# Two attention blocks on one core, planned by a list scheduler: a correction for every job, eviction and value round in the plan's ranking

## The chip, the cores and the metric

The kernel runs on one core of a Trainium2 chip. The metric is the device time in microseconds of one execution, the median of several runs. A profile of one execution stands beside it: its span is the time from the first to the last instruction of the program, and its own device time is a little longer.

## The reference

Two attention blocks of 2048 tokens, width 1024 and 32 heads of 32, in bf16, side by side in the output. The core of it, with the transposes left out:

```python
# A: plain attention over 2048 keys
qkv = x @ wqkv                                   # q, k, v: 32 heads x 2048 x 32
p = softmax(q @ k.T * Dh ** -0.5)
a = (p @ v) @ wo
# B: four segments of 512 with a memory carried along
for s in range(4):
    p = softmax(qs @ ks.T * scale + causal_mask)
    o = g * (phi(qs) @ M) / (phi(qs) @ z + 1e-6) + (1 - g) * (p @ vs)
    M = M + phi(ks).T @ vs;  z = z + phi(ks).sum()
b = concat(o) @ wo
out = concat(a, b)
```

## The kernel before

**Operations.** Attention A goes in 8 groups of 4 heads, each in 8 blocks of 256 queries; attention B in 4 segments, each in pairs of groups. The unit of work is a *set*: one tile of scores for each of 4 heads, 128 keys by 512 columns.

- A *row set* (L966) is the score matmuls of a set on TensorE (PE): four heads at a time in four row strips of the array. It is marked `urgent`.
- Two *exps* (L1042) on ScalarE (ACT) turn the set's scores into P, two tiles (1024 columns) at a time, from PSUM to a ring of 20 tiles in SBUF. `SLOT_BANKS` gives three slots of two PSUM banks; a set fills two slots, and each exp frees one.
- In about four of eight sets of a block (`SQUARES`) one of the four tiles takes another way: VectorE (DVE) writes Y (L1003), GpSimd (POOL) squares it into Pc (L1006), and the first exp has 512 columns only.
- A *value round* (`round`, L1133 and L1140) multiplies the tiles of a set by V and by ones, four heads at a time in four column strips: pairs of steps of 256 columns, which gather in one PSUM bank for a block. When an exp wants a tile of the ring, the last value step that reads the tile's old contents must have ended.
- A *norm* on DVE and POOL (L1191 to L1274) divides by the sums.
- *Jobs* are the projections: Q and K (`job_KA`, `job_KB`), V (`job_VA`, `job_VB`), outputs (`job_outA`, `job_outB`, and for the last rows `job_part`, `job_whole`, `job_last`), the memory of B (`job_phi`, `job_mem`, `job_M`) and some guards. A projection is eight steps of 512 columns (L599 is `mm4`, the helper that issues a step's four matmuls), each of which the plan may cut into two halves, and then an *eviction* by DVE (L1347). Jobs and value rounds share the PSUM banks 6 and 7 (`POOL_BANKS`).
- K and Q are squared on POOL (L1361) for a bound on the scores.

**Order.** Every operation is first recorded as an `Op` with its engine, a planned duration, a key (its wished place on a time axis in the plan), and its dependencies; `build` calls the recorded items in order of key. Then `Prog.schedule`, a list scheduler, plays all engines through and writes down one fixed order for each; `emit` sets the semaphores. Nothing is decided at run time but a guard against large scores. On each engine but PE, the ready operation with the smallest key comes first; what reads a group's PSUM bank has `XR` taken off its key, and an urgent operation that is ready soon enough (`SOON`) goes ahead. On PE, `pick` takes a row set when it is due (`ROW_LEAD`), and otherwise the operation with the smallest rank: for a value round its number `pvn` against the exps opened so far (`PV_ROOM`, `PV_T`, `PV_HOT`), for a job its key against the exps' progress (`JOB_AT`, `JOB_SLOPE`) or its due time (`DUE_AT`, `DUE_SLOPE`), with deductions for staying in one tiling mode (`STICK`) and for a group that is open (`XC`). A job is a candidate only up to `AHEAD` before its key. Weight loads go out from SyncE (SP), each gated by an exp.

```python
def rank(x):
    if x.pvn is not None:
        k = (x.pvn + PV_ROOM - st["opn"]) * PV_T if st["rows"] and x.need - st["opn"] > PV_HOT else -100.0
    else:
        k = JOB_AT + JOB_SLOPE * max(min(x.key - st["prog"], 20.0), -20.0)
        k = min(k, DUE_AT + DUE_SLOPE * (x.due - st["prog"]))
    if x.mode == mode:
        k -= STICK
    if x.grp is not None and x.pvn is None and not opens(x):
        k -= XC
    return k, x.key
```

Of the kernel before, what the change touches and what calls it, by code (L numbers as in the profile page):

```python
# [7 lines left out]
ACT = mybir.ActivationFunctionType  # L8
ALU = mybir.AluOpType
# [12 lines left out]
QC = 256  # L22
SLOT_BANKS = ((0, 1), (2, 3), (4, 5))
POOL_BANKS = (6, 7)
OL_LEAD, OL_MAX = 3.677, 7.166
P_RING = 20
Y_RING, C_RING = 3, 4
T_RING = 3
# [8 lines left out]
SQUARE_PV = 0.574  # L37
WHOLE = (("A", 7, 7), ("A", 7, 6))
BCK = 12.877
SOON = 0.596  # L40

PAIR = ((6, 0), (6, 1), (6, 2), (7, 0), (7, 1), (7, 2), (7, 3), (6, 3), (7, 4), (6, 4), (7, 5), (6, 5), (6, 6), (7, 6), (6, 7), (7, 7))
BIAS_PART = (17, 16, 18)
# [85 lines left out]
class Op:  # L129
    __slots__ = ("eng", "fn", "dur", "lat", "key", "mode", "svc", "deps", "order", "sem", "semval", "inc", "count",  # L130
                 "start", "end", "users", "ready", "urgent", "sched", "heat", "prog", "pvn", "margin", "pos", "due", "grp",
                 "gate", "alt", "flag", "redo", "need", "both")

    def __init__(self, eng, fn, dur, lat, key, mode=None, sem=None):
        self.eng, self.fn, self.dur, self.lat, self.key, self.mode, self.sem = eng, fn, dur, lat, key, mode, sem
# [9 lines left out]


LAT = {"PE": 0.22, "ACT": 0.29, "DVE": 0.10, "POOL": 0.15, "SP": 0.1}
SWITCH = 0.10
WIN = 3.413
ROW_LEAD = 2.689  # L150
AHEAD = 9.68
HEAT = 0.897
STICK = 0.28
OVER = 2.794
PV_ROOM = 6.219
PV_T = 1.014
PV_HOT = 1.215
NORM_K = 6.738
JOB_AT = 0.5
JOB_SLOPE = 0.572  # L160
MARGIN = 4.491
RXJ = 4
RX0 = 34.374
LEAD_A, LEAD_B, DUE_AT, DUE_SLOPE = 10.658, 3.249, 14.476, 0.203
HOLD = {}
BACKLOG = 3.378
XR = 9.514
XC = 2.115
STEP = 1.599
OUT3 = 90.167  # L170
OT_STEP = 3
NUDGE = {('KB', 3, 1): 15, ('VB', 1, 1): 4.2, ('OB', 0, 0): 5.05, ('OA', 1): 15, ('OB', 2, 0): 12, ('KB', 1, 0): 10.93, ('OA', 4): -21.65, ('KA', 5): -3.8, ('KB', 3, 2): 2.84, ('OA', 3): -6.14, ('OA', 5): 2.94, ('VB', 0, 0): -25, ('phi', 3, 1): 7.4, ('KB', 3, 3): 2.86, ('KB', 2, 2): -1.94, ('OA', 0): 4.63, ('VB', 2, 0): 8.32, ('phi', 0, 1): 2.89, ('KB', 1, 1): -15.35, ('phi', 1, 1): 2.05, ('phi', 3, 3): -0.06, ('VB', 1, 0): -1.48, ('OB', 0, 1): 8.97, ('VB', 2, 1): 3.43, ('OB', 3, 0): 6.01, ('VB', 3, 1): -7.84, ('OB', 1, 1): 2.06, ('OB', 1, 0): 6.22, ('KB', 1, 2): -2.71, ('phi', 0, 0): 4.5, ('VB', 0, 1): 10.96, ('OB', 3, 1): 7.23, ('phi', 2, 2): 5.96, ('KB', 2, 1): 13.45, ('VA', 1): -2.83, ('KA', 2): -0.38, ('KB', 2, 0): -4.38, ('phi', 2, 3): 0.21, ('phi', 3, 0): 0.15, ('phi', 0, 2): -2.66, ('phi', 1, 2): -2.16, ('phi', 2, 1): 5.51, ('OA', 2): 6.02, ('phi', 0, 3): -5.66, ('KB', 1, 3): -4.93, ('phi', 1, 0): 0.24, ('KB', 0, 1): 3.02, ('KB', 2, 3): -10.8, ('phi', 3, 2): 4.76, ('KA', 4): -4.63, ('phi', 1, 3): 15, ('KB', 0, 3): 10.75, ('KB', 0, 0): 3.13, ('VA', 3): -2.83, ('KB', 3, 0): -3.52, ('phi', 2, 0): -0.06, ('KA', 3): -0.02, ('OB', 2, 1): 6.93, ('VB', 3, 0): 0.3, ('KB', 0, 2): -0.5, ('KA', 6): -1.58}
SAFE = 0
WOA_STEP = 2
OUT_D = 66.251
M_AT = 1.576
# [6 lines left out]
class Prog:  # L183
    def __init__(self):
        self.ops = []
        self.due = 1e9
        self.before = {}

    def op(self, eng, fn, dur, key, reads=(), writes=(), mode=None, sem=None, lat=None, after=()):
        o = Op(eng, fn, dur, LAT[eng] if lat is None else lat, key, mode, sem)  # L190
        o.due = self.due
        for r in reads:
            for x in r.w:
                self._dep(o, x, True)
        for r in writes:
            for x in r.w:
                self._dep(o, x, False)
            for x in r.r:
                self._dep(o, x, False)
        for x in after:  # L200
            self._dep(o, x, True)
        for r in reads:
            r.r.append(o)
        for r in writes:
            r.w, r.r = [o], []
        for g in {r.grp for r in (*reads, *writes) if r.grp is not None}:
            o.grp = g
            if eng == "PE" and g.pe:
                o.order.add(g.pe[0])
            (g.pe if eng == "PE" else g.rd).append(o)  # L210
        self.ops.append(o)
        return o
# [13 lines left out]
    def schedule(self):  # L226
# [11 lines left out]
        for o in self.ops:  # L238
            al = o.deps | o.order | {x for x, _ in o.gate}
            pend[o] = len(al)  # L240
            for x in al:
                x.users.append(o)
        exps = {o: n for n, o in enumerate(o for o in self.ops if o.prog)}
        for o in self.ops:
            if o.pvn is not None:
# [14 lines left out]
        last = {b: list(r.w) + list(r.r) for b, r in self.before.items()}  # L260
# [45 lines left out]
        def pick(t, av, c):  # L306
            mode = st["mode"]
            row = [x for x in av if x.urgent]
            nxt = [x for x in c if x.urgent]
            due = max(min((x.ready for x in nxt), default=1e9), st["act_end"] - ROW_LEAD) if nxt else 1e9  # L310
            if row and t >= due - 0.02:
                return min(row, key=lambda x: x.key)
            slack = due - t
            cold = heat(t, 2.6) < HEAT * 2.6
            def rank(x):
# [9 lines left out]
                return k, x.key  # L325
            av = [x for x in av if not x.urgent and (x.pvn is not None or x.key <= st["prog"] + AHEAD or cold)]
            first = [min((x for x in av if opens(x) and x.grp.sums is v), key=rank, default=None) for v in (False, True)]
            best = None
            for x in av:
                if opens(x) and x not in first:  # L330
                    continue
                d = x.dur + (SWITCH if x.mode != mode else 0.0)
                v = (d > slack + OVER, *rank(x))
                if best is None or v < best[0]:
# [9 lines left out]
        while left:  # L344
            best = None
            for e, c in cand.items():
                if c:
                    t = max(free[e], min(x.ready for x in c))
                    if best is None or t < best[0]:
                        best = (t, e)  # L350
            t, e = best
            c = cand[e]
            av = [x for x in c if x.ready <= t + 1e-9]
            if e == "PE":
                av = [x for x in av if not opens(x) or opening(x)[0] <= t + 1e-9]
                o = pick(t, av, c)
                if o is None:
# [6 lines left out]
                    o = min((x for x in c if x.ready <= t + 1e-9 and (not opens(x) or opening(x, True)[0] <= t + 1e-9)), key=lambda x: x.key)  # L364
            else:
                if e == "SP" and st["dma"] - t > BACKLOG:
# [5 lines left out]
                    c = av  # L372
                o = min((x for x in c if x.ready <= t + HOLD.get(e, 0.0)), key=lambda x: x.key - (XR if x.grp is not None else 0.0))
                soon = min((x for x in c if x.urgent), key=lambda x: x.ready, default=None)
                if soon is not None and soon.ready < max(t, o.ready) + o.dur - SOON:
                    o = soon
                t = max(t, o.ready)
            d = o.dur
            if e == "PE":
                ck = clock(t)  # L380
                d /= ck
                if o.mode != st["mode"]:
                    t += SWITCH
                st["mode"] = o.mode
# [182 lines left out]
class _Kernel:  # L567
# [63 lines left out]
    def build(self):  # L631
        nc = self.nc
        with ExitStack() as es:
            self.es = es
            self.alloc()
            self.items = []
            self.exps, self.exp_keys = [], []
            self.plan()
            self.items.sort(key=lambda x: (x[0], x[1]))
            for key, _, f in self.items:  # L640
                f(key)
            self.pg.before = {b: self.bank[b] for b in POOL_BANKS}
            self.pg.schedule()
            run = self.pg.emit(nc, es, None, self.out_sems + self.sm_last)
            block = es.enter_context(nc.Block())

            @block.gpsimd
            def _(eng):
                run("POOL", eng)

            @block.sync
            def _(eng):
                run("SP", eng)

            @block.tensor
            def _(eng):
                run("PE", eng)

            @block.scalar
            def _(eng):  # L660
                run("ACT", eng)

            @block.vector
            def _(eng):
                run("DVE", eng)
# [325 lines left out]
    def plan_square(self, t, bank, T):  # L991

        i, k = self.nsquare % Y_RING, self.nsquare % C_RING
        self.nsquare += 1
        Y, rY = self.Y[i], self.r_Y[i]
        dst, rP = self.Pc[:, k, :], self.r_Pc[k]
        t["P"] = (self.Pc, k, rP)
        bc = t["bias"]
        last = []

        def f(key):
            src = self.ps[:, 512 * bank:512 * bank + 512]
            o = self.dve(lambda e: e.tensor_scalar(Y[:, :], src, KAPPA * SCALE, BETA, ALU.mult, ALU.add), 512, key - 9.0,  # L1003
                         [self.bank[bank]], [rY], fixed=0.15)
            o.urgent = True
            last.append(self.pool(lambda e: e.tensor_tensor(dst, Y[:, :], Y[:, :], ALU.mult), 512, key - BCK, [rY], [rP], rate=0.435))  # L1006
        self.item(T + 0.001, f)
        return (lambda e: e.activation(dst, Y[:, :], ACT.Exp, bias=self.bias[:, 60 + bc:61 + bc], scale=1.0 / KAPPA),
                bc, rY, rP, last, t)
# [347 lines left out]
    def square(self, kind, src, rsrc, key):  # L1357
        i = self.nsq[kind] % 4
        self.nsq[kind] += 1
        sq, rs = self.sq[kind][i], self.r_sq[kind][i]  # L1360
        self.pool(lambda e: e.tensor_tensor(sq[:, :], src, src, ALU.mult), 512, key, [rsrc], [rs], rate=0.5)  # L1361
        return sq, rs

    def guard_cols(self, key, sqs, bank=None, urgent=None, wide=512):
# [648 lines left out]
```

## Time and profile before

| | |
|---|---|
| time, median of 3 runs | 1090.2 us (1090.05 to 1095.13) |
| profiled execution | 1089.23 us, its span 1087.5 us |
| granted TensorE clock | 0.999 |
| PE busy (matmuls) | 1027.5 us, 25410 instructions |
| ACT busy | 1030.8 us, 1224 instructions |
| DVE busy | 734.4 us, 1648 instructions |
| POOL busy | 575.3 us, 653 instructions |
| exps (L1042) | 1176, 1001.5 us |

Busy times are the union of an engine's instructions in the profiled execution; matmuls are pipelined, so PE's share is not a share of its peak. In rows of a timeline the columns are start and duration in us, engine, line, operation, out<-in, shapes and count, with the idle time before and what ended it in brackets. In rows of groups they are busy us and mean ns of one, then the idle time before and its releasers. In rows of waits they are the total in us, how often, and the longest.

### The profile page before, as it was taken

How to read it: one execution, taken by the hardware profiler on the slowest of the kernel's cores; microseconds unless marked ns; L12 is line 12 of the kernel's file. 1: busy time of each engine (PE TensorE's matmuls, PEld its weight loads, DVE VectorE, ACT ScalarE, POOL GpSimd, SP SyncE). 2: the span in 40 equal slices, each digit the busy share in tenths (PEclk: the TensorE clock that was granted, in tenths of full speed). 3: DMA queues.
4: the chain of work that ended last, by engine and by line, in shares of the span. 5: the costliest groups of instructions: out<-in, count | busy, mean ns of one | idle time of the engine just before them, and what ended most of it. 6: DMA issues, size and time to landing. Idle time of an engine off the chain costs nothing.

```text
span 1087.5 us, 56100 instructions
## 1 busy us (share of the span) xinstructions
PE 1027.5 (94%) x25410; PEld 560.7 (52%) x25410; DVE 734.4 (68%) x1648; ACT 1030.8 (95%) x1224; POOL 575.3 (53%) x653
## 2 busy tenths in 40 slices
PE   8999999999999999998989999999999999999998
PEld 4555555655545544465445544466555545445554
DVE  2346587578585587887685598786865697774444
ACT  4999999999999999998999999999999999999997
POOL 2213575457564475756456476665646567554311
PEclk9999999999999999999999999999999999999999
DMA  9032251016223240033212241042112551021201
GB/s 196 22 88 56 65 139 31 9 16 121 52 63 100 69 97 20 13 59 85 56 50 80 66 107 23 15 95 55 47 34 71 134 191 42 31 68 45 67 27 51
DMA packets 171391, 72.18 MB, mean 66 GB/s; under 512 B 134800, under 2 KB 169360, under 8 KB 171152
## 3 DMA queue, kind: packets, MB, share of 16 engines
q1 hardware_dynamic: 168784, 67.79, 25.4%
q8 instruction: 200, 3.28, 1.3%
q10 hardware_dynamic: 2368, 0.79, 0.3%
q14 instruction: 39, 0.32, 0.1%
HBM read 45.29 MB, written 11.73 MB: 52 GB/s over the span
## 4 chain that ended last, share of the span: by engine, by line
PE 62%; ACT 21%; DVE 11%; issue 2%; SPq 2%; DMA 1%; POOL 0%; ACTq 0%; DVEq 0%
PE ps L599 31%; ACT P L1042 20%; PE ps L966 12%; PE ps L1133 9%; PE ps L1140 8%; DVE Y L1003 2%; SPq L1312 2%; DVE T L1191 1%; PE ps L1602 1%; DVE PKQ_B L1651 1%; ACT PKQ_B L1646 1%; DVE KQ_B L1347 1%; DMA xT_A<-in_A_x_dram 1%; DVE rc L1202 1%; DVE T L1197 1%
## 5 line engine op out<-in xcount | busy, mean ns | idle before, releaser
L1042 ACT ACTIVATE P<-ps 128x1024 bf16<-128x1024 f32 (+1 forms) x1176 | 1001.5, 996 | 36.8 <-PE ps L1140 16.1
L1006 POOL TENSOR_TENSOR Pc<-Y 128x512 bf16<-128x512 f32 x226 | 238.5, 1055 | 255.1 <-DVE Y L1003 102.3
L1140 PE MATMUL ps<-P,onesb 128*32 128x256 bf16 (+1 forms) x4412 | 295.0, 270 | 0.3 <-issue 0.3
L1133 PE MATMUL ps<-P,V_A 128*32 128x256 bf16 x3644 | 252.4, 274 | 4.6 <-DVE T L1197 1.3
L966 PE MATMUL ps<-KQ_A 32*128 32x256 bf16 x4096 | 204.0, 273 | 18.5 <-ACT P L1042 10.3
L1003 DVE TENSOR_SCALAR Y<-ps 128x512 f32<-128x512 f32 x226 | 154.4, 683 | 79.8 <-PE ps L966 73.1
L966 PEld LDWEIGHTS ps<-KQ_A 32*128 32x128 bf16 x4096 | 61.9, 92 | 161.3 <-ACT P L1042 99.6
L599 PE MATMUL ps<-xT_B,W_B 128*32 128x512 bf16 (+1 forms) x2244 | 138.6, 362 | 4.6 <-DVE OT_B L1672 1.6
L1140 PEld LDWEIGHTS ps<-P,onesb 128*32 128x32 bf16 x4412 | 129.2, 97 | 24.5 <-issue 9.5
L599 PE MATMUL ps<-xT_A,W_A 128*32 128x512 bf16 (+1 forms) x2224 | 138.1, 364 | 3.7 <-DMA xT_A<-in_A_x_dram 1.1
L1133 PEld LDWEIGHTS ps<-P,V_A 128*32 128x32 bf16 x3644 | 107.7, 96 | 36.4 <-issue 11.9
L1133 PE MATMUL ps<-Pc,V_A 128*32 128x256 bf16 x452 | 112.9, 273 | 0.4 <-ACT P L1042 0.2
L1140 PE MATMUL ps<-Pc,onesb 128*32 128x256 bf16 x452 | 113.2, 273 | 0.0
L1361 POOL TENSOR_TENSOR sqA<-KQ_A 128x512 bf16<-128x512 bf16 x61 | 64.7, 1063 | 85.8 <-DVE KQ_A L1347 44.2
L1065 POOL TENSOR_SCALAR_AFFINE_SELECT P<-P 128x768 bf16<-128x768 bf16 (+1 forms) x96 | 77.7, 814 | 48.0 <-ACT P L1042 47.0
L1361 POOL TENSOR_TENSOR sqB<-KQ_B 128x512 bf16<-128x512 bf16 x64 | 68.1, 1063 | 38.6 <-DVE KQ_B L1347 27.7
L1191 DVE STREAM_TRANSPOSE T<-ps 128x256 f32<-128x256 f32 (+1 forms) x148 | 71.8, 486 | 23.6 <-PE ps L1140 19.5
L599 PEld LDWEIGHTS ps<-xT_B,W_B 128*32 128x32 bf16 x2244 | 51.5, 96 | 55.8 <-issue 23.3
L599 PEld LDWEIGHTS ps<-xT_A,W_A 128*32 128x32 bf16 x2224 | 51.7, 96 | 50.2 <-issue 15.3
L1347 DVE CAST KQ_A<-ps 128x512 bf16<-128x512 f32 x60 | 41.1, 686 | 48.6 <-PE ps L599 48.6
L1213 DVE STREAM_TRANSPOSE T<-rc 128x256 f32<-128x256 f32 (+1 forms) x152 | 71.6, 477 | 1.8
L1347 DVE CAST outsb<-ps 128x512 bf16<-128x512 f32 x56 | 38.4, 686 | 50.2 <-PE ps L599 40.7
(113 smaller groups left out, 1305.8 us busy)
## 6 DMA issues: line engine op xcount, KB each, us to landing
Wv_B<-in_B_wv_dram SPq DMA_DIRECT2D x32, 256.0 KB, 3.2
W_B<-in_B_wk_dram SPq DMA_DIRECT2D x32, 256.0 KB, 3.2
W_B<-in_B_wq_dram SPq DMA_DIRECT2D x32, 256.0 KB, 3.8
Wo_B<-in_B_wo_dram SPq DMA_DIRECT2D x32, 256.0 KB, 3.0
out_dram<-outsb SPq DMA_DIRECT2D x56, 128.0 KB, 1.8
W_A<-in_A_wqkv_dram SPq DMA_DIRECT2D x14, 256.0 KB, 3.2
ot_a_scratch<-OTst SPq DMA_DIRECT2D x51, 64.0 KB, 1.9
xT_A<-ot_a_scratch SPq DMA_DIRECT2D x6, 512.0 KB, 4.7
```

The lines of the kernel that those rows point to most:

```text
L599: ins = e.matmul(out[r], w[:, r], x, start=start, stop=stop, tile_position=(0, 32 * t), skip_group_check=True)
L966: ins = e.matmul(out, kap, qap, start=st, stop=True, tile_position=(32 * h, 0), skip_group_check=True)
L1003: o = self.dve(lambda e: e.tensor_scalar(Y[:, :], src, KAPPA * SCALE, BETA, ALU.mult, ALU.add), 512, key - 9.0, [self.bank[bank]], [rY], f ...
L1006: last.append(self.pool(lambda e: e.tensor_tensor(dst, Y[:, :], Y[:, :], ALU.mult), 512, key - BCK, [rY], [rP], rate=0.435))
L1042: a = self.act(guarded if early else lambda e: e.activation(dst, src, ACT.Exp, scale=SCALE), cols, key, rd, wr, fixed=EXP_FIXED)
L1065: self.pool(lambda e: e.affine_select(v, v, pattern=pat, compare_op=ALU.is_ge, fill=0.0, base=0, channel_multiplier=-1), 2 * nd * P, key + ...
L1133: ins = e.matmul(self.pb(obk, q0, q0 + nq, slice(32 * h, 32 * h + 32)), v, p, start=first, stop=last, tile_position=(0, 32 * h), skip_grou ...
L1140: ins = e.matmul(self.pb(obk, QC + q0, QC + q0 + nq, slice(32 * h, 32 * h + 32)), self.onesb[:, 0:32], p, start=False, stop=last, tile_pos ...
L1191: self.dve(lambda e: e.transpose(T2[:, 0:n], src()), n, nk, rsrc, [r2], fixed=0.17)
L1213: self.dve(lambda e: e.transpose(T2[:, 0:n].rearrange("p (b r) -> p b r", r=32), bc), n, key, [rr], [r2], fixed=0.17)
L1347: self.dve(lambda e: e.tensor_copy(dst, src()), 512, key, [self.at(b)], rdst, fixed=0.155)
L1361: self.pool(lambda e: e.tensor_tensor(sq[:, :], src, src, ALU.mult), 512, key, [rsrc], [rs], rate=0.5)
```

## The change

Two things change in what the planner is given, and nothing in what is computed. Every recorded `Op` gets the number of the item that made it, and before the scheduling starts a table `SHIFT`, with 1638 entries by item and engine, is added to its key, or for a value round to its number `pvn`; row sets and exps have none. Seventeen of the planner's constants get other values, and two planned rates of POOL's squares go from 0.435 and 0.5 to 0.56 elements per ns. The counts of operations on every engine stay the same; twelve projection steps more than before are issued as two halves.

```diff
-OL_LEAD, OL_MAX = 3.677, 7.166
+OL_LEAD, OL_MAX = 4.319064149904418, 41.00003697785312
-SOON = 0.596
+SOON = 0.5905590911714352
-ROW_LEAD = 2.689
-AHEAD = 9.68
-HEAT = 0.897
-STICK = 0.28
-OVER = 2.794
-PV_ROOM = 6.219
-PV_T = 1.014
-PV_HOT = 1.215
+ROW_LEAD = 10.450797042452189
+AHEAD = 122.90457192896793
+HEAT = 2.917270822004343
+STICK = -2.216533454202848
+OVER = 9.83100976449197
+PV_ROOM = 6.511791041192874
+PV_T = 1.226406207969171
+PV_HOT = 1.9091538080027601
-JOB_AT = 0.5
-JOB_SLOPE = 0.572
+JOB_AT = 1.1168622049752417
+JOB_SLOPE = 1.811535016666137
-LEAD_A, LEAD_B, DUE_AT, DUE_SLOPE = 10.658, 3.249, 14.476, 0.203
+LEAD_A, LEAD_B, DUE_AT, DUE_SLOPE = 10.658, 3.249, 49.75785267190463, 1.9998068229774686
-XR = 9.514
-XC = 2.115
+XR = 67.02011029255661
+XC = 2.943398126899734
+SHIFT = {(n, e): v for e, t in (
+    ("POOL", {
+        3: -0.5, 4: 1.5, 5: 0.25, 6: 3, 8: 1.75, 10: -4.5, 11: -0.5, 12: 2.75, 13: 3.25, 15: 0.5, 16: 1.25, 17: 5.5,
...
+) for n, v in t.items()}
@@ Prog.op
         o.due = self.due
+        o.item = self.item
@@ Prog.schedule, ahead of everything that uses a key
+        for o in self.ops:
+            if o.pvn is not None:
+                o.pvn += SHIFT.get((o.item, o.eng), 0.0)
+            elif not o.prog and (o.urgent is None or o.eng != "PE"):
+                o.key += SHIFT.get((o.item, o.eng), 0.0)
@@ _Kernel.build
-            for key, _, f in self.items:
+            for key, n, f in self.items:
+                self.pg.item = n
                 f(key)
@@ plan_square
-            last.append(self.pool(lambda e: e.tensor_tensor(dst, Y[:, :], Y[:, :], ALU.mult), 512, key - BCK, [rY], [rP], rate=0.435))
+            last.append(self.pool(lambda e: e.tensor_tensor(dst, Y[:, :], Y[:, :], ALU.mult), 512, key - BCK, [rY], [rP], rate=0.56))
@@ square
-        self.pool(lambda e: e.tensor_tensor(sq[:, :], src, src, ALU.mult), 512, key, [rsrc], [rs], rate=0.5)
+        self.pool(lambda e: e.tensor_tensor(sq[:, :], src, src, ALU.mult), 512, key, [rsrc], [rs], rate=0.56)
```

More of the change, by code (lines that the diff above doesn't have):

```diff
@@ L131 @@
                  "start", "end", "users", "ready", "urgent", "sched", "heat", "prog", "pvn", "margin", "pos", "due", "grp",
-                 "gate", "alt", "flag", "redo", "need", "both")
+                 "gate", "alt", "flag", "redo", "need", "both", "item")
     def __init__(self, eng, fn, dur, lat, key, mode=None, sem=None):
@@ L147 @@
 LAT = {"PE": 0.22, "ACT": 0.29, "DVE": 0.10, "POOL": 0.15, "SP": 0.1}
-SWITCH = 0.10
+SWITCH = 0.1
 WIN = 3.413
-ROW_LEAD = 2.689
-AHEAD = 9.68
-HEAT = 0.897
-STICK = 0.28
-OVER = 2.794
-PV_ROOM = 6.219
-PV_T = 1.014
-PV_HOT = 1.215
+ROW_LEAD = 10.450797042452189
[6 more added lines that the diff above has]
+PV_HOT = 1.9091538080027601
 NORM_K = 6.738
-JOB_AT = 0.5
-JOB_SLOPE = 0.572
+JOB_AT = 1.1168622049752417
+JOB_SLOPE = 1.811535016666137
 MARGIN = 4.491
@@ L172 @@
 NUDGE = {('KB', 3, 1): 15, ('VB', 1, 1): 4.2, ('OB', 0, 0): 5.05, ('OA', 1): 15, ('OB', 2, 0): 12, ('KB', 1, 0): 10.93, ('OA', 4): -21.65, ('KA', 5): -3.8, ('KB', 3, 2): 2.84, ('OA', 3): -6.14, ('OA', 5): 2.94, ('VB', 0, 0): -25, ('phi', 3, 1): 7.4, ('KB', 3, 3): 2.86, ('KB', 2, 2): -1.94, ('OA', 0): 4.63, ('VB', 2, 0): 8.32, ('phi', 0, 1): 2.89, ('KB', 1, 1): -15.35, ('phi', 1, 1): 2.05, ('phi', 3, 3): -0.06, ('VB', 1, 0): -1.48, ('OB', 0, 1): 8.97, ('VB', 2, 1): 3.43, ('OB', 3, 0): 6.01, ('VB', 3, 1): -7.84, ('OB', 1, 1): 2.06, ('OB', 1, 0): 6.22, ('KB', 1, 2): -2.71, ('phi', 0, 0): 4.5, ('VB', 0, 1): 10.96, ('OB', 3, 1): 7.23, ('phi', 2, 2): 5.96, ('KB', 2, 1): 13.45, ('VA', 1): -2.83, ('KA', 2): -0.38, ('KB', 2, 0): -4.38, ('phi', 2, 3): 0.21, ('phi', 3, 0): 0.15, ('phi', 0, 2): -2.66, ('phi', 1, 2): -2.16, ('phi', 2, 1): 5.51, ('OA', 2): 6.02, ('phi', 0, 3): -5.66, ('KB', 1, 3): -4.93, ('phi', 1, 0): 0.24, ('KB', 0, 1): 3.02, ('KB', 2, 3): -10.8, ('phi', 3, 2): 4.76, ('KA', 4): -4.63, ('phi', 1, 3): 15, ('KB', 0, 3): 10.75, ('KB', 0, 0): 3.13, ('VA', 3): -2.83, ('KB', 3, 0): -3.52, ('phi', 2, 0): -0.06, ('KA', 3): -0.02, ('OB', 2, 1): 6.93, ('VB', 3, 0): 0.3, ('KB', 0, 2): -0.5, ('KA', 6): -1.58}
-SAFE = 0
+SAFE = 0.0
+SHIFT = {(n, e): v for e, t in (
+    ("POOL", {
[42 rows of a table added]
+    ("DVE", {
[132 rows of a table added]
+    ("ACT", {
[3 rows of a table added]
+) for n, v in t.items()}
 WOA_STEP = 2
@@ L186, in __init__ @@
         self.due = 1e9
+        self.item = 0
         self.before = {}
```

176 rows, old and new, of the table SHIFT are left out of this document.

## The prediction

> **What bounds the kernel now.** I read the page first: its busy shares, slices, chain and costliest group.
>
> ```profile
> span 1087.5 us, 56100 instructions
> ...
> PE 1027.5 (94%) x25410; PEld 560.7 (52%) x25410; DVE 734.4 (68%) x1648; ACT 1030.8 (95%) x1224; POOL 575.3 (53%) x653
> ...
> PE   8999999999999999998989999999999999999998
> ACT  4999999999999999998999999999999999999997
> PEclk9999999999999999999999999999999999999999
> ...
> PE 62%; ACT 21%; DVE 11%; issue 2%; SPq 2%; DMA 1%; POOL 0%; ACTq 0%; DVEq 0%
> ...
> L1042 ACT ACTIVATE P<-ps 128x1024 bf16<-128x1024 f32 (+1 forms) x1176 | 1001.5, 996 | 36.8 <-PE ps L1140 16.1 <-PE ps L966 14.1 <-PE ps L1602 1.4
> ```
>
> ACT and PE are both nearly full all the time, at an undisturbed clock, and the chain changes between them: they run in lockstep. PSUM has three slots of two banks; a row set (L966) fills two of them and two exps (L1042) empty them, so PE can be ahead of ACT by a fraction of one exp only. No instruction is added or taken away by the change, so ACT's 1030.8 us of work stay. What can go are ACT's waits. The sums by stretch say how many there are away from both ends:
>
> ```profile
> 50.00:1075.00 1025.00, 975.07 (x24356) 533.89 (x24344) 713.46 (x1599) 991.27 (x1181) 562.44 (x611) 1.00 0.25 64
> ```
>
> 1025.00 - 991.27 = 33.7 us. The waits of ACT say on what (total, times, longest):
>
> ```profile
> ACT P L1042 <- PE ps L1140: 16.1, 28, 1.3
> ACT P L1042 <- PE ps L966: 14.1, 36, 2.5
> ACT KQ_A L1517 <- PE ps L599: 8.1, 1, 8.1
> ACT P L1029 <- DVE flags L1450: 3.5, 1, 3.5
> ACT P L1042 <- PE ps L1133: 1.1, 1, 1.1
> ```
>
> Two kinds count. An exp waits for its **row set** (L966, 14.1 us): PE came to it too late. Or it waits for a **value round** (L1140 and L1133, 17.2 us): the exp writes a tile of the ring P, and the round that still reads this tile stands further back in PE's order. The 8.1 and 3.5 us belong to the start; both programs are alike there (PE's first 171 steps, to the ninth row set). The timeline around 460 us shows the second kind.
>
> ```profile
> 459.86 2.18 ACT L1042 ACTIVATE P<-ps 128x1024 bf16<-128x1024 f32 x2
> ...
> 460.57 0.40 PE L966 MATMUL ps<-KQ_A 32*128 32x256 bf16 x8
> 460.90 1.26 PE L599 MATMUL ps<-xT_A,W_A 128*32 128x512 bf16 x20
> 461.99 0.28 PE L1133 MATMUL ps<-P,V_A 128*32 128x256 bf16 x4
> 462.10 0.28 PE L1140 MATMUL ps<-P,onesb 128*32 128x256 bf16 x4
> ...
> 462.31 0.40 PE L966 MATMUL ps<-KQ_A 32*128 32x256 bf16 x8
> 462.64 0.29 PE L1133 MATMUL ps<-P,V_A 128*32 128x256 bf16 x3
> ...
> 462.98 0.28 PE L1140 MATMUL ps<-P,onesb 128*32 128x256 bf16 x3
> ...
> 463.31 1.02 ACT L1042 ACTIVATE P<-ps 128x1024 bf16<-128x1024 f32 x1 [1.27 <-PE ps L1140]
> ```
>
> After the row set at 460.57 PE does five projection steps, a pair of value steps, the next row set, and only then the value steps that free the tile. The second exp of the set of 460.57 stands still for 1.27 us, though its scores were ready long before.
>
> The same rows give prices. Five projection steps (20 matmuls of 512 columns) take from 460.90 to 461.99, 0.218 each; a value step (four matmuls of 256 columns) takes 461.99 to 462.10, 0.11; a row set 462.31 to 462.64, 0.33, and about 0.11 between the last value step's share and its start, so 0.44. The exps:
>
> ```profile
> 29.05 1.02 ACT L1042 ACTIVATE P<-ps 128x1024 bf16<-128x1024 f32 x1
> 40.10 4.69 ACT L1042 ACTIVATE P<-ps 128x1024 bf16<-128x1024 f32 x5 [0.16 <-PE ps L1140]
> L1042 ACT ACTIVATE P<-ps 128x1024 bf16<-128x1024 f32 x950 | 924.6, 1078 | 30.4 <-PE ps L1140 14.3 <-PE ps L966 9.9 <-PE ps L1602 1.4
> L1042 ACT ACTIVATE P<-ps 128x512 bf16<-128x512 f32 x226 | 146.4, 648 | 6.4 <-PE ps L966 4.2 <-PE ps L1140 1.8
> ```
>
> One alone shows 1.02, five in a row 4.69: (4.69 - 1.02) / 4 = 0.917 from start to start. The 512-column one is shorter by 1078 - 648 ns, so 0.487.
>
> **The change part by part.** I laid the two programs' orders side by side and counted in both with these prices; no clock of the plan enters.
>
> *Value rounds.* For each exp I took the value step that frees its tile and summed PE's steps between the exp's own row set and that step; it is late where the sum is over 0.2 us (a first exp; from the row set's end at 460.90 to its exp at about 461 lies a little less) or 0.2 plus the first exp's length (a second exp). Before: 48 exps late, 19.8 us together, 1.5 of it in one set of the start. The trace has 17.2 us, and the late places are those of its long waits (the one above is counted at 1.05). After: 20 late, 6.7 us, the same 1.5 included. At the places that hold six of the long waits of before, the freeing step now stands ahead of the next row set. Scaled, 17.2 x 6.7 / 19.8 = 5.8 stay: **-11.4 us**. The best case is that only the start's 1.5 stay, -15.7; the worst is rival 2.
>
> *Jobs and row sets.* Between two row sets PE has what ACT takes from the end of one set's first exp to the end of the next set's: 0.917 + 0.917, or 0.917 + 0.487 where the next set has a square, and a phi exp if one lies there. I summed PE's steps in each of 582 gaps (those of the start left out) with 0.44 for the row set. The mean gap is 0.06 us under ACT's time in both orders, but the spread is smaller after (standard deviation 0.34 before, 0.26 after). What exceeds ACT's time by over 0.3 us, counted beyond the 0.3: before 65 gaps with 14.9 us, after 36 with 5.2. All excess: before 46.1, after 25.9. The first count is near the measured 14.1, the second far above, so I take the first: 14.1 x 5.2 / 14.9 = 4.9 stay, **-9.2 us**. By the second 7.9 would stay, -6.2; none can give more than -14.1.
>
> *The end.* It grows.
>
> ```profile
> 1078.38 1.47 PE L599 MATMUL ps<-V_A,xT_A 128*32 128x512 bf16 x24
> 1080.21 0.61 PE L599 MATMUL ps<-V_A,xT_A 128*32 128x512 bf16 x8
> 1080.64 2.52 PE L599 MATMUL ps<-W_A,xT_A 128*32 128x512 bf16 x40
> 1081.64 0.42 DVE L1252 TENSOR_TENSOR xT_A<-ps,T 128x256 bf16<-128x256 f32 x1
> ```
>
> The last output sums have fourteen steps; six (the row at 1078.38) stand ahead of the last value steps and eight behind them, from 1080.21. Then come four that need what DVE delivers at 1082.06 (1081.64 + 0.42). Eight at 0.218 end at 1081.95: just hidden. In the new order an output job stands behind the last row set and pushes these steps back: two are ahead of the last value steps, twelve behind, and one of job_last among them. Thirteen end at 1080.21 + 2.83 = 1083.04. An eviction now stands in the last normalisation on DVE too; it moves DVE's end by less than that. **+1.0 us**; from 0 to +1.7.
>
> *The rest.* The two planning rates of POOL (0.435 and 0.5, now 0.56 elements per ns) alter no instruction. They tell the plan 512 / 0.56 + 150 = 1064 ns for a square, where the row has 1055; the old 0.435 gave 1327.
>
> ```profile
> L1006 POOL TENSOR_TENSOR Pc<-Y 128x512 bf16<-128x512 f32 x226 | 238.5, 1055 | 255.1 <-DVE Y L1003 102.3 <-PE ps L599 60.0 <-ACT P L1042 24.6
> ...
> PE ps L599 <- issue: 2.7, 2, 2.4
> ...
> PE ps L1372 <- POOL P L1065: 0.4, 1, 0.4
> ...
> W_B<-in_B_wq_dram SPq DMA_DIRECT2D x32, 256.0 KB, 3.8
> ```
>
> Twelve more projection steps are cut into halves of 256 columns; the halves cost what the whole does. Openings of the two shared banks (6 and 7) that come before the eviction is over are 42 instead of 50 by the same count. The weight loads of B take 3.8 us to land (the row above) and by the order still have at least a set's time, some 1.7 us, to spare. One stall of 2.4 us within a job waits for nothing in the order; I leave it in and give it to the range.
>
> Sum: -11.4 - 9.2 + 1.0 = -19.6. The profiled execution took 1089.2 (1.7 outside its span), 1.0 under the median of 1090.2; the sum is relative, so 1090.2 - 19.6 = 1070.6.
>
> **The rivals.**
>
> *1. PE becomes the bound.* 0.06 us x 592 sets is 36 us of room on PE, hardly more than ACT's 33.7 us of waits. If drains that my prices miss eat it, the row sets stay as late as they are, and -11.4 + 1.0 gives 1079.8. For it: PE's 94%. Against it: ACT's row waits came from single long gaps, not from all. The Trainium skill (Perfetto Trace Analysis, Identifying the Most-Contended Engine) judges PE's room by its weight-load share and not by matmul busy time; by the 52% here this rival would give nothing back. The trace bears out that busy time misleads, but not a room of half: the gaps have 0.06 us.
>
> *2. The ring is too small, not badly ordered.* Twenty tiles of P stay twenty. If PE frees tiles later than its order says, the waits for value rounds only move, and -9.2 + 1.0 gives 1082.0. Against it: the count by order hits the waits of before one by one. The Trainium skill (Perfetto Trace Analysis, Optimization Strategy) has this rule: the same gap again and again on the engine that should be full can mean that SBUF has too few buffers. By it the 17.2 us stay. The trace shows 29 waits on nearly 1200 exps, not a steady gap.
>
> *3. Slower: squares come late to PE.* The value steps of a squared tile wait for POOL. Those within three sets of their row set are 70 instead of 58, which is 35 squares at two pieces each. PE takes its steps in order, so each late square stops the row sets behind it. Late by one POOL instruction each, 35 x 1.055 = 37 us are added: 1107.5. It outweighs the gain from 19 such squares on. Against it: PE's waits in the trace have no row for Pc, only 0.4 us for POOL, at a similar spacing, and POOL is 53% busy.
>
> *4. Nothing changes.* The plan's order is right for the plan's clock only, and waits appear elsewhere (banks, loads) as fast as they go: about 1090. Against it: I counted with measured prices.
>
> **How the numbers follow.** Forecast 0.62, rival 1 0.12, rival 2 0.13, rival 3 0.06, rival 4 0.07. Low end: the ring's best case, -15.7 - 9.2 + 1.0, and the 2.4 us stall gone: 1063.9. High end: rival 2 with one more such stall, 1084.4. So 1064 to 1084 leaves out rivals 3 and 4 and a little of the others. What a measurement of this kernel can tell is about 0.5%, 5.5 us: the forecast and rivals 1 and 2 are faster by more (0.87), rival 4 is the same (0.07), rival 3 slower (0.06).
>
> **What would show it.** In ACT's waits after: L1140 and L1133 together near 6 us (rival 2: near 17), L966 near 5 (rival 1: near 14), ACT's busy time unchanged near 1031. In the timeline of the end: the last four projection steps a microsecond later after the last exp. Rival 3 would show as PE waiting for POOL Pc. ACT busy by 10 us more or less, or a new releaser of over 8 us in ACT's waits, would prove the account wrong.

## The result, and the profile after

The changed kernel takes **1308.7 us** (median of 4 runs, 1305.57 to 1311.95) against 1091.6 us for the kernel before (4 runs): a ratio of 1.198, interval 1.194 to 1.203. The forecast was 1070.6 us, with a chance of 0.06 on slower. The profiled execution took 1311.95 us, 1310.2 of it in the span. All lines of the code after the new table stand 190 lower: the exps are L1232 instead of L1042, their guarded form L1219 instead of L1029, row sets L1156, value rounds L1323 and L1330.

The page of the changed kernel, in the parts shown of before:

```profile
span 1310.2 us, 56408 instructions
...
PE 1069.0 (82%) x25458; PEld 567.0 (43%) x25458; DVE 731.8 (56%) x1648; ACT 1262.4 (96%) x1450; POOL 576.0 (44%) x653
...
PE   8988888888888877887778778888777887888887
...
ACT  4999999999999999999999999999999999999997
...
PEclk9998999999999999999999999999999999999999
...
ACT 44%; PE 6%; POOL 4%; issue 2%; DVE 1%; POOLq 0%; DVEq 0%; ACTq 0%
```

The count at the end of ACT's entry is the first thing to read: 1450 instructions where before had 1224, so 226 more, and 1262.4 us of work instead of 1030.8. That is +231.6 us busy; the span grew by 1310.2 - 1087.5 = 222.7, so ACT even waits 8.9 us less. The loss is work on ACT, not a wait. The lockstep of before is gone too: the chain changed between PE (62%) and ACT (21%), and now ACT leads it.

ACT's groups, by line and shape:

```profile
L1219 ACT ACTIVATE P<-ps,bias 128x1024 bf16<-128x1024 f32 x934 | 1001.0, 1209 | 12.7 <-PE ps L1156 8.1 <-PE ps L788 4.3 <-PE ps L1330 0.2
L1198 ACT ACTIVATE Pc<-Y,bias 128x512 bf16<-128x512 f32 x226 | 188.5, 836 | 13.6 <-POOL Pc L1196 13.6
L1219 ACT ACTIVATE P<-ps,bias 128x512 bf16<-128x512 f32 x226 | 182.5, 808 | 2.0 <-PE ps L1156 2.0
L1232 ACT ACTIVATE P<-ps 128x1024 bf16<-128x1024 f32 x24 | 22.5, 1053 | 3.0 <-PE ps L1792 1.4 <-PE ps L1330 1.2 <-PE ps L1615 0.5
```

Before, 1176 exps stood on the plain line and 8 on the guarded one. Now 1160 are guarded, those 8 among them, with a bias operand (`ps,bias`) that the plain form lacks, and 226 instructions of a kind that before did not run at all compute each squared tile once more on ACT (`Pc<-Y,bias`). The timeline of ACT says when it begins:

```profile
45.68 6.55 ACT L1232 ACTIVATE P<-ps 128x1024 bf16<-128x1024 f32 x7
53.07 10.15 ACT L1219 ACTIVATE P<-ps,bias 128x1024 bf16<-128x1024 f32 x10 [0.83 <-PE ps L788]
...
91.43 0.95 ACT L1198 ACTIVATE Pc<-Y,bias 128x512 bf16<-128x512 f32 x1
92.04 3.35 ACT L1219 ACTIVATE P<-ps,bias 128x1024 bf16<-128x1024 f32 x3
```

So from 53 us on, after the first 8 and 24 plain exps, ACT runs another stretch of program. `emit` writes ACT's stream twice (`run_split`): ACT loads a flag, and if it is set it branches to a copy of all that follows, in which each exp takes its guarded form and is preceded by the redone squares of its set. From that copy there is no way back. How often ACT loads a flag tells which copy it is in. The groups of the tile `flags`, of the kernel before and of the changed one:

```profile
L557 ACTq TENSOR_LOAD <-flags x24: 273/278/476, 24.3 to 960.2; - x24
```

```profile
L746 ACTq TENSOR_LOAD <-flags x2: 285/376/467, 27.3 to 50.1; - x2
```

Before, 24 loads up to 960 us, and none branched. After, the second load, at 50.1 us, is the last: the branch is taken there. In the rest of this document this count stands for the flag: 24 is down, 2 is up.

**Why the flag goes up.** The inputs are the same. A guard bounds the scores from squares of K and Q: matmuls sum the squares into a PSUM bank, 32 rows for each 512-column tile, and DVE takes the maximum over the columns (`cols`), then bound and flag. The third guard and the fifth (at 36.5 and 74.1 us) are given two tiles, the other early ones four:

```python
ins = e.matmul(self.pb(b, 0, wide, slice(32 * c, 32 * c + 32)), ...)       # c over the tiles: rows 0 to 63 for two
o = self.dve(lambda e: e.tensor_reduce(self.cols[:, ci:ci + 1], self.pb(b, 0, wide), AX.X, ALU.max), wide, ...)   # all rows
self.guard_more(key, self.sqA[(0, 0)], 1, *BIAS_PART[1:])                  # sqA[(0, 0)] has two tiles
```

The trace of the changed kernel shows it (timeline of PE and DVE; the count at the end of a matmul's row is its strips):

```profile
36.49 0.39 PE L1562 MATMUL ps<-sqA,blk 128*32 128x512 bf16 x2
...
36.92 0.69 DVE L1569 TENSOR_REDUCE cols<-ps 128x1 f32<-128x512 f32 x1 [1.12 <-PE ps L1562]
...
40.42 0.15 DVE L1640 SCALAR_TENSOR_TENSOR flags<-braw,flags 128x1 int32<-128x1 f32 x1
...
54.90 0.39 PE L1562 MATMUL ps<-sqA,blk 128*32 128x512 bf16 x4
```

Two matmuls fill 64 rows, and the reduce reads 128. The other 64 hold what the bank's last user left. In the order of before the third guard opens bank 7 at row set 10, behind a projection job of row set 8, and the fifth stands behind a projection too, before and after. In the new order the third guard's own correction of -3.25 on PE, among the others, puts it at row set 9 into bank 6, behind a value round of row set 7. That leaves sums of exps over many keys, and the threshold (`FREE`) on the bound is 0.1. Flags are chained by a maximum, so once one is up all later ones are. That was the theory; the trace does not name banks (they are read off the planned order) and shows no values.

### The profile page after: what moved, and what is told of

Read it like the earlier page. It is cut to its first block, busy times and chain, and to the rows that moved or that the text cites. A ratio compares the mean times of both kernels' runs of the same rounds, so it can differ in the third digit from the quotient of the medians.

```text
span 1310.2 us, 56408 instructions
## 1 busy us (share of the span) xinstructions
PE 1069.0 (82%) x25458; PEld 567.0 (43%) x25458; DVE 731.8 (56%) x1648; ACT 1262.4 (96%) x1450; POOL 576.0 (44%) x653
## 3 DMA queue, kind: packets, MB, share of 16 engines
q1 hardware_dynamic: 168784, 67.79, 20.9%
## 4 chain that ended last, share of the span: by engine, by line
ACT 44%; PE 6%; POOL 4%; issue 2%; DVE 1%; POOLq 0%; DVEq 0%; ACTq 0%
ACT P L1219 39%; ACT Pc L1198 5%; POOL Pc L1196 3%; PE ps L788 3%; PE ps L1156 2%; PE ps L1323 1%; ACT PKQ_B L1836 1%; PE ps L1330 1%; DVE Y L1193 1%; POOL T L1463 0%; POOL OT_B L1464 0%; POOL sqA L1551 0%; POOL sqB L1551 0%; DVE T L1403 0%; POOL OTst L1449 0%
## 5 line engine op out<-in xcount | busy, mean ns | idle before, releaser
L1219 ACT ACTIVATE P<-ps,bias 128x1024 bf16<-128x1024 f32 (+1 forms) x1160 | 1116.7, 1131 | 14.7 <-PE ps L1156 10.0
L1156 PE MATMUL ps<-KQ_A 32*128 32x256 bf16 x4096 | 205.8, 275 | 164.8 <-ACT P L1219 149.4
L1330 PE MATMUL ps<-P,onesb 128*32 128x256 bf16 (+1 forms) x4412 | 298.0, 272 | 0.1
L1323 PE MATMUL ps<-P,V_A 128*32 128x256 bf16 x3644 | 257.2, 276 | 2.0 <-ACT P L1219 1.4
L1156 PEld LDWEIGHTS ps<-KQ_A 32*128 32x128 bf16 x4096 | 63.9, 93 | 334.0 <-ACT P L1219 273.2
L1198 ACT ACTIVATE Pc<-Y,bias 128x512 bf16<-128x512 f32 x226 | 188.5, 836 | 13.6 <-POOL Pc L1196 13.6
L1323 PE MATMUL ps<-Pc,V_A 128*32 128x256 bf16 x452 | 115.0, 278 | 38.3 <-ACT P L1219 37.3
L788 PE MATMUL ps<-xT_A,W_A 128*32 128x512 bf16 (+1 forms) x2276 | 141.3, 361 | 3.1 <-DMA xT_A<-in_A_x_dram 2.7
L1330 PEld LDWEIGHTS ps<-P,onesb 128*32 128x32 bf16 x4412 | 129.3, 97 | 24.3 <-issue 9.4
L1323 PEld LDWEIGHTS ps<-P,V_A 128*32 128x32 bf16 x3644 | 108.0, 97 | 31.4 <-issue 11.7
L1330 PE MATMUL ps<-Pc,onesb 128*32 128x256 bf16 x452 | 115.4, 277 | 0.0
L788 PEld LDWEIGHTS ps<-xT_B,W_B 128*32 128x32 bf16 x2208 | 51.7, 97 | 50.3 <-issue 21.3
```

What stands on the lines that cost most here:

```text
L788: ins = e.matmul(out[r], w[:, r], x, start=start, stop=stop, tile_position=(0, 32 * t), skip_group_check=True)
L1156: ins = e.matmul(out, kap, qap, start=st, stop=True, tile_position=(32 * h, 0), skip_group_check=True)
L1219: guarded = lambda e: e.activation(dst, src, ACT.Exp, bias=self.bias[:, bc:bc + 1], scale=SCALE)
L1323: ins = e.matmul(self.pb(obk, q0, q0 + nq, slice(32 * h, 32 * h + 32)), v, p, start=first, stop=last, tile_position=(0, 32 * h), skip_grou ...
L1330: ins = e.matmul(self.pb(obk, QC + q0, QC + q0 + nq, slice(32 * h, 32 * h + 32)), self.onesb[:, 0:32], p, start=False, stop=last, tile_pos ...
```

## The experiments

**What the other branch costs.** The kernel before with one flag forced up, nothing else:

```diff
-  scalar=-FREE, in1=self.flags[:, nf:nf + 1], op0=ALU.is_lt, op1=ALU.max), 1,
+  scalar=0.0 if nf == 2 else -FREE, in1=self.flags[:, nf:nf + 1], op0=ALU.is_lt, op1=ALU.max), 1,
```

> The kernel before with the third guard's flag raised at any bound (threshold 0 instead of -0.1), so that the old order goes down the guarded branch from the same place on. Theory 1: ACT's work becomes that of the changed kernel, 1262 us and 40 to 50 us of waits: 1290 to 1325 us. If a part of the loss came from the new order, it stays clearly below 1290 us.

Measured: 1315.4 us, ratio 1.203 (1.200 to 1.205). Its groups on ACT are those of the changed kernel:

```profile
L1029 ACT ACTIVATE P<-ps,bias 128x1024 bf16<-128x1024 f32 x934 | 1000.4, 1203 | 16.6 <-PE ps L1140 6.2 <-PE ps L966 6.1 <-DVE flags L1450 3.5
L1008 ACT ACTIVATE Pc<-Y,bias 128x512 bf16<-128x512 f32 x226 | 185.8, 825 | 15.3 <-POOL Pc L1006 13.3 <-PE ps L1140 1.1 <-PE ps L1133 0.8
```

The branch by itself makes the whole loss. Whether the new order is worth anything in it can't be told: the ratios of the two kernels to the kernel before, 1.198 (1.194 to 1.203) and 1.203 (1.200 to 1.205), have intervals that overlap. Then the changed kernel in its guarded branch, but leaving the squared tiles as POOL made them:

```diff
-                    for redo, _, _, _, (c,), _ in fix:
-                        e.wait_ge(self.pg.sems["POOL"], c.count)
-                        redo(e)
```

> The changed kernel with the guarded branch taken, but without the redoing of squared tiles by ACT in it: the 226 tiles keep POOL's squares (that part of the computation is left out). It splits the guarded branch's price. By the trace of the changed kernel a redone tile takes ACT 0.61 us from start to start (91.43 to 92.04), 138 us in all, and ACT's waits for POOL's Pc are 13.6 us: 1308 - 152 = 1156 us. If the bias operand of the ordinary exps is the whole price, it stays near 1308 us; if the redone tiles are the whole price, it falls to 1071 to 1090 us.

Measured: 1149.8 us (ratio 1.052, 1.050 to 1.054; expected 1156). The busy times of its page:

```profile
PE 1047.5 (91%) x25458; PEld 561.4 (49%) x25458; DVE 733.9 (64%) x1648; ACT 1120.2 (98%) x1224; POOL 575.8 (50%) x653
```

The redone squares are 1308.7 - 1149.8 = 159 us, 0.70 us each with their waits for POOL (13.6 us in the changed kernel). What is left over the same order with plain exps (1069.3, below) is 80.5 us, for the 1152 exps that have a bias operand here and none there. ACT's busy time differs by more, 1120.2 - 1025.3 = 94.9 us or 0.082 us for each of them; ACT's waits went down meanwhile, from 42.2 to 27.0 us (span less busy time).

**What raises the flag.** If it is the unwritten rows, then writing them is enough. The changed kernel with the guard's two tiles taken twice, so that four strips fill all 128 rows, and the fifth's as well; bank and place stay (bank 6, row set 9):

```diff
-        self.guard_more(key, self.sqA[(0, 0)], 1, *BIAS_PART[1:])
+        self.guard_more(key, 2 * self.sqA[(0, 0)], 1, *BIAS_PART[1:])
...
-        self.guard_more(key, self.sqA[(0, 1)], None, None, 0)
+        self.guard_more(key, 2 * self.sqA[(0, 1)], None, None, 0)
```

> The new order, untouched, but the two guard matmuls of group 0 (guard_A0, guard_A0q) also write the lower half of their bank's rows, with the same squares again: four strips instead of two. Theory 1 (the guard's maximum read rows 64 to 127 that an older value round had left in its bank, and so sent all later exps down the guarded branch): no guarded exp after the first 8, no redone square on ACT, ACT busy back near 1031 us, and the time that the order alone gives, by the prediction's account 1070.6 us (1064 to 1084). Rival theory 2 (the guard is right, because the new order reads K or Q too early, or the exps are long for another reason): the guarded exps stay and so do about 1308 us. Rival theory 3 (the guard was the stale rows', but the order brings nothing): guarded exps gone, 1085 to 1095 us.

Measured: **1069.3 us** (1066.55 to 1071.15), ratio 0.978 (0.976 to 0.980). From its page, its timeline, its groups and its waits:

```profile
PE 1023.8 (96%) x25462; PEld 559.6 (52%) x25462; DVE 730.6 (68%) x1648; ACT 1025.3 (96%) x1224; POOL 577.2 (54%) x653
```

```profile
36.83 0.40 PE L1562 MATMUL ps<-sqA,blk 128*32 128x512 bf16 x4
```

```profile
L746 ACTq TENSOR_LOAD <-flags x24: 273/278/474, 27.6 to 939.8; - x24
```

```profile
ACT P L1232 <- PE ps L1156: 9.5, 26, 0.9
...
ACT P L1232 <- PE ps L1330: 4.7, 11, 1.2
...
ACT P L1219 <- PE ps L1156: 3.4, 2, 2.9
```

Four matmuls more (x25462 instead of x25458), and 239 us less. The same edit in the kernel before is the control:

> The kernel before with the same four strips. All theories: as before within 0.3 %, since only two times two matmuls of 0.22 us beside others are added; it is the control for what the strips cost.

Measured: 1090.6 us, ratio 0.998 (0.996 to 0.999): where the left-over rows do no harm, writing them changes next to nothing.

The strips could have helped in another way than by the rows they fill. So the next run leaves two strips and moves the guard away from bank 6, by taking out its own correction on PE:

```diff
+SHIFT.pop((2919, "PE"))
```

> Changed kernel with one of its 1,638 corrections taken out: that of the third guard's own TensorE item, (2919, PE). The guard keeps its two strips. Planned order: the guard then opens bank 7 with row set 10, which only prologue projections have used, in place of bank 6 with row set 9, behind a value round. Theory 'left-over rows' (the reduce reads 64 rows that the guard did not write, and what the bank's last user left there decides the flag): flag stays down, plain exps on the later line, no second squares on ACT; the rest of the order is nearly the changed kernel's (21 value rounds late by 9.3 us in my count against 20 by 6.7, gaps beyond 0.3 us 35 summing to 6.7 us against 36 and 5.2), so 1069 + about 4 = 1073 us, between 1068 and 1082. Rival 'the two added strips themselves changed the plan or the data, not the rows they fill': one correction less changes nothing of it, about 1309 us.

Measured: 1068.9 us (1067.75 to 1070.91), ratio 0.978 (0.976 to 0.981). All lines stand one lower again. The guard still has two strips, in bank 7 behind a projection job of row set 8 (not of the prologue, as the expectation has it), and the flag is down:

```profile
36.65 0.39 PE L1563 MATMUL ps<-sqA,blk 128*32 128x512 bf16 x2
```

```profile
L747 ACTq TENSOR_LOAD <-flags x24: 273/278/473, 24.4 to 938.4; - x24
```

One number among 1,638 makes 240 us, and it is the guard's. The reverse: the kernel before, without any correction or new constant, with only this guard moved 5 us ahead in its key, which puts it into bank 6 behind a value round there (the fifth guard then stands behind one as well).

```diff
-        add(1.0, p2 - 4.0, 0.4, lambda key: self.guard_A0(key + 2.0))
+        add(1.0, p2 - 4.0, 0.4, lambda key: self.guard_A0(key - 3.0))
```

> Kernel before, everything as it was but the third guard's key 5 us earlier (key - 3.0 in place of key + 2.0). In the old order this moves the guard from bank 7 (row set 10) to bank 6 (row set 9), behind a value round of row set 7. No correction, no new constant. Theory 'left-over rows': the flag goes up and the kernel runs its guarded branch from there: as the kernel before with the flag forced, 1315 us, within 10. Rival 'the flag needs the new order of the squares or of the other guards': plain exps, 1091 to 1095 us (count of late value rounds 53 by 23.9 us against 48 by 19.8, so +3).

Measured: 1313.5 us, ratio 1.203 (1.199 to 1.206). The old order fails in the same way:

```profile
34.49 0.38 PE L1372 MATMUL ps<-sqA,blk 128*32 128x512 bf16 x2
```

```profile
L557 ACTq TENSOR_LOAD <-flags x2: 288/379/470, 25.2 to 48.0; - x2
```

The same early guard with four strips:

> Kernel before with the third guard 5 us earlier (bank 6 behind a value round, as in the run that went to 1313.5 us) and with four strips in place of two. Planned order as that run's: 53 value rounds late by 23.9 us against 48 by 19.8 before, gaps beyond 0.3 us 66 summing to 18.2 us against 65 and 14.9. Theory 'left-over rows': flag down, 24 flag loads, and the time of the kernel before plus what its late value rounds give: with the ratios of the first runs (0.75 to 0.87 us per counted us) 3 to 4 us, so 1094 to 1097 us. Rival 'an early guard in bank 6 raises the flag whatever it writes': about 1313 us.

Measured: 1093.5 us, ratio 1.001 (0.999 to 1.002), expected 1094 to 1097: the flag is down, and the time is not to be told from that of the kernel before.

```profile
L557 ACTq TENSOR_LOAD <-flags x24: 274/278/469, 24.7 to 965.0; - x24
```

Last, the other side of the fault. The guard keeps two strips in bank 6 behind the value round, PE does nothing more, and only the read is narrowed to what was written (the other 64 rows take over the maximum so far):

```diff
+        h = 32 * len(sqs)
-        ... e.tensor_reduce(self.cols[:, ci:ci + 1], self.pb(b, 0, wide), AX.X, ALU.max) ...
+        ... e.tensor_reduce(self.cols[:h, ci:ci + 1], self.pb(b, 0, wide, slice(0, h)), AX.X, ALU.max) ...
...
+        if h < P:
+            o = self.dve(lambda e: e.tensor_copy(self.cols[h:, ci:ci + 1], self.cols[h:, c0:c0 + 1]), 1, key + 0.1, [r0], [rc])
```

> Changed kernel, third guard in bank 6 behind the value round and with its two strips, as in the changed kernel; nothing is added on TensorE. Only its read is narrowed: the reduce takes the 64 rows that the two strips wrote, and the running maximum of the other 64 rows is carried over by one copy of one column (some 0.15 us on VectorE). Planned order: 21 value rounds late by 7.3 us, gaps beyond 0.3 us 37 summing to 5.5 us, as the changed kernel's within 0.6 us. Theory 'left-over rows': the flag stays down, plain exps, 24 flag loads, 1069 to 1071 us. Rival 'the two strips' own values are over the threshold, or what stands in bank 6 harms the strips themselves': the flag goes up as before, about 1309 us.

Measured: **1067.3 us** (1065.8 to 1069.1), ratio 0.976 (0.974 to 0.979), the lowest median here, though not to be told from the other two of the new order with the flag down, and a little under the 1069 to 1071 us expected. Its timeline:

```profile
33.75 0.39 PE L1562 MATMUL ps<-sqA,blk 128*32 128x512 bf16 x2
...
34.18 0.68 DVE L1570 TENSOR_REDUCE cols<-ps 64x1 f32<-64x512 f32 x1 [1.02 <-PE ps L1562]
34.90 0.15 DVE L1589 COPY cols<-cols 64x1 f32<-64x1 f32 x1
```

```profile
L746 ACTq TENSOR_LOAD <-flags x24: 273/278/475, 24.6 to 939.8; - x24
```

The runs stand in a square, in both orders:

| guard's bank, rows written of those read | old order | new order |
|---|---|---|
| bank 7 behind a projection, 64 of 128 | 1091.6 (before) | 1068.9 |
| bank 6 behind a value round, 64 of 128 | **1313.5** | **1308.7** (changed kernel) |
| bank 6 behind a value round, 128 of 128 | 1093.5 | 1069.3 |
| bank 6 behind a value round, 64 of 64 | | 1067.3 |

The flag goes up where both come together: a bank that a value round has just left, and rows that are read but not written. The two strips' own values are innocent (last row). Two things are not shown: the values in the unwritten rows, which no trace has, and the number of the bank apart from its last user, since both change together in these runs. The Trainium skill (PSUM — Partial Sum Buffer, The four PSUM rules) says that bytes which a matmul doesn't write keep their old data, readable by VectorE; the square agrees.

**The forecast's own terms.** With the flag down, which part of the change brings the gain? Both parts alone, with four strips: the new constants with an empty table (`SHIFT = {}`), and the table with the old constants. POOL's two planned rates keep their new values in both.

> Changed kernel with four guard strips (flag down), the new constants, and the table of corrections empty. Counted in the planned order as in the prediction: 64 value rounds late by 30.0 us (before 48 by 19.8, changed 20 by 6.7), 75 row-set gaps beyond 0.3 us summing to 17.8 us (before 65 by 14.9, changed 36 by 5.2). Theory 'the corrections carry the gain and the constants alone are no better than the old ones': 1090.2 + 17.2*(30.0-19.8)/19.8 + 14.1*(17.8-14.9)/14.9 = 1102 us, between 1094 and 1112. Rival 'the constants bring part of the gain': below 1087 us.

> Changed kernel with four guard strips (flag down), the old constants, and the table of corrections as changed. Count: 69 value rounds late by 40.3 us, 72 gaps beyond 0.3 us summing to 22.4 us. Theory 'corrections fit only the constants they were made beside': 1090.2 + 17.2*(40.3-19.8)/19.8 + 14.1*(22.4-14.9)/14.9 = 1115 us, between 1100 and 1130. Rival 'the corrections bring the gain by themselves': 1069 to 1080 us.

Measured: 1097.5 us for the constants alone (ratio 1.0035, 1.002 to 1.005), 1102.4 for the table alone (1.008, 1.0055 to 1.011). Each alone is a little slower than before, together they are 2.2% faster: of the two sets of constants, the table helps with the one that it goes with. The signs were as expected, the sizes smaller (expected 1102 and 1115, with the kernel before at 1090.2; beside these runs it took 1093.3). ACT's waits of the two:

```profile
ACT P L1233 <- PE ps L1331: 23.1, 44, 1.8
...
ACT P L1233 <- PE ps L1157: 6.2, 16, 1.0
...
ACT P L1233 <- PE ps L1324: 1.6, 2, 1.1
```

```profile
ACT P L1232 <- PE ps L1330: 30.5, 38, 2.9
ACT P L1232 <- PE ps L1156: 8.6, 24, 1.2
```

The waits of three more runs, with the guard's own correction out, with the narrowed read, and of the old order with the early guard and four strips:

```profile
ACT P L1233 <- PE ps L1157: 8.3, 23, 1.6
...
ACT P L1233 <- PE ps L1331: 8.0, 15, 2.0
```

```profile
ACT P L1232 <- PE ps L1156: 11.1, 30, 1.0
...
ACT P L1232 <- PE ps L1330: 6.0, 14, 1.2
```

```profile
ACT P L1042 <- PE ps L1140: 20.9, 29, 1.9
ACT P L1042 <- PE ps L966: 14.3, 32, 1.7
```

Beside the counts by order (us), with the two lines of value rounds taken together:

| kernel | late value rounds: count, measured | gaps over 0.3: count, row-set waits measured |
|---|---|---|
| before | 19.8, 17.2 | 14.9, 14.1 |
| changed, four strips | 6.7, 4.7 | 5.2, 9.5 |
| changed, read narrowed | 7.3, 6.0 | 5.5, 11.1 |
| changed, own correction out | 9.3, 8.0 | 6.7, 8.3 |
| constants alone | 30.0, 24.7 | 17.8, 6.2 |
| table alone | 40.3, 30.8 | 22.4, 8.6 |
| before, guard early, four strips | 23.9, 20.9 | 18.2, 14.3 |

The first count orders all seven kernels, and the measured waits are 0.70 to 0.87 of it. The waits for row sets do not follow the second count.

## Why the prediction was wrong

**The step that failed** stands in the first paragraph: "No instruction is added or taken away by the change, so ACT's 1030.8 us of work stay." It holds for the program and not for what is run of it: ACT's stream is written twice, and which copy runs is decided by data. The same goes for "nothing in what is computed" in the account of the change. ACT's work became 1262.4 us. That "ACT busy by 10 us more or less" would prove the account wrong was the right thing to watch, but no chance was given to it: none of the four rivals was the other branch, though all pieces lay open in the code. There was a line for 8 guarded exps at the start of the trace of before, a flag load on ACT, a branch in `run_split`. The prediction even counted the openings of banks 6 and 7 in both orders, for stalls; it did not ask what an opening finds in the bank.

**The rivals.** Rival 3, the only one on the slower side, had squares that come late from POOL: 1107.5 us. In the run with four strips, PE's waits name POOL Pc with 0.5 us in all:

```profile
PE ps L1323 <- POOL Pc L1196: 0.5, 2, 0.3
```

Rival 2 (the ring is too small) had the value-round waits stay near 17; with the ring as it was they fell to 4.7 by order alone. Rival 4 (nothing changes) has no run on its side. Rival 1 (row-set waits stay near 14) is right in part: they fell, but to 9.5 and not to 4.9.

**The terms, with the flag down** (four strips against before):

- Value rounds: forecast 17.2 to 5.8, measured 4.7. The count was right in size and, over seven orders, in rank.
- Row sets: forecast 14.1 to 4.9, measured 9.5. This term of the sum gave half of what was forecast, 4.6 instead of 9.2. That the count lay near 14.1 for the kernel before, the reason for taking it, was luck: for the constants alone it gives 14.1 x 17.8 / 14.9 = 16.8 and the trace 6.2. Why a long gap often costs nothing was not tried; where an exp is already held by a value round, PE has time to catch up, but that is argued only.
- The end: forecast +1.0. The last exps end at 1079.71 of 1087.5 us before and at 1058.80 of 1067.5 with four strips, so 7.8 and 8.7 us: +0.9, as forecast. ACT's timelines of the two:

```profile
1069.36 10.35 ACT L1042 ACTIVATE P<-ps 128x1024 bf16<-128x1024 f32 x11
```

```profile
1043.85 14.95 ACT L1232 ACTIVATE P<-ps 128x1024 bf16<-128x1024 f32 x16
```

- The sum: forecast -19.6, measured 1069.3 - 1090.6 = -21.3 against the control with the same strips. The two kinds of wait and the end give -12.5 - 4.6 + 0.9 = -16.2 of the 20.0 by which the spans differ. The profiled run with four strips also waited 3.0 us longer at its start (3.4 instead of 0.4 us for a row set), and ACT was busy 5.5 us less, 1025.3 instead of 1030.8: -18.7, with 1.3 left open. The smaller busy time was not forecast. An exp that begins alone shows 1.02 where one in a row adds 0.917, and there are 28 waits fewer of the two kinds (37 instead of 65); by this estimate they make 2.9 of the 5.5. That the sum came out near the forecast is thus in part luck: the row sets gave 4.6 us less than forecast, and ACT's smaller busy time took their place.

So the forecast mechanism is there with the flag down, its value rounds and its end at the forecast size and its row sets at half of it, and 239 us of another one lie on top of it.

## What to carry to other kernels

Where a program has branches, "no instruction is added" says nothing of the instructions that run: look for operations in the code that do not occur in the trace, and ask what data would call them. A change of order alone may change data wherever something reads more than was written just before it, so compare for each partly filled buffer not only when it is opened but who held it last. When the count of instructions of an engine changes against the plan, read that number before any wait.

## What the runs showed of the hardware

A bias operand on an exp from PSUM is not free: without the redone squares, 1152 exps with one instead of none made ACT busy for 94.9 us more, 0.082 us each, and the kernel 80.5 us longer. The means of the rows can't be used for this, since rows overlap: for the 1024-column exp they differ by 1325 - 1107 = 218 ns between the same two runs. The Trainium skill (ScalarE: Activation LUTs, What ACT_TABLE_LOAD costs) gives about 93 ns for each pointer operand; by that an estimate is 107 us for 1152 of them. The measured 94.9 us is near it, and decides here.

The taken branch itself shows as one short gap. In the changed kernel the last plain exp ends at 45.68 + 6.55 = 52.23 us and the first guarded one begins at 53.07 (row shown above): 0.83 us idle, which its row puts down to a PE step. The three other runs that branch have 0.68, 0.84 and 0.85 there (flag forced, no redo, early guard), and those that do not branch run through, as in the same order with four strips:

```profile
46.04 15.71 ACT L1232 ACTIVATE P<-ps 128x1024 bf16<-128x1024 f32 x17
```

Against the 239 us of what the branch leads to, this gap is small. A flag load takes 278 ns by its median; 24 of them stand in the plain stream, and in the run with four strips no wait of ACT is put down to one.
